# A new prologue, phi(k) ahead of its transpose, and DMA transposes in a fused attention and token-mixing kernel

## The chip, the core and the metric

The kernel runs on one core of a Trainium2 chip. A core has five instruction queues: TensorE (matmuls, PE in the profile), VectorE (DVE), ScalarE (ACT), GpSimd (POOL) and SyncE (SP, which here only issues transfers). They run independently and meet at semaphores. Transfers run on 16 DMA engines shared by all queues. Matmuls write PSUM, which has 8 banks of 128 x 512 float32; everything else lives in SBUF.

The metric is the device time of one execution in microseconds. The profile adds one profiled execution, whose span (first to last instruction) is a little shorter than its device time.

## What is computed

A residual block over 2048 tokens of width 1024: `x + A(layernorm(x)) + B(layernorm(x))`, all in bfloat16.

```python
def _A_ref(x, wq, wk, wv, wo, beta):            # 32 heads of 32, 4 segments of 512 tokens
    ...
    phi = lambda t: jnp.where(t > 0, t + 1.0, jnp.exp(t))
    ...
    for s in range(N):
        qs, ks, vs = (q[:, :, s].copy(), k[:, :, s].copy(), v[:, :, s].copy())
        logits = jnp.einsum('bhqd,bhkd->bhqk', qs, ks) * scale + mask
        p = _softmax(logits, axis=-1)
        a_dot = jnp.einsum('bhqk,bhkd->bhqd', p, vs)
        pq = phi(qs)
        num = jnp.einsum('bhld,bhde->bhle', pq, M)
        den = jnp.einsum('bhld,bhd->bhl', pq, z)[..., None] + 1e-06
        a_mem = num / den
        o = g * a_mem + (1.0 - g) * a_dot
        outs.append(o)
        pk = phi(ks)
        M = M + jnp.einsum('bhld,bhle->bhde', pk, vs)
        z = z + jnp.einsum('bhld->bhd', pk)
    ...
    return o @ wo

def _B_ref(x, w1, b1, w2, b2):
    h = _layernorm(x, axis=-1)
    u = jnp.einsum('bsd,sf->bdf', h, w1) + b1    # sums over the 2048 tokens, 3584 hidden
    u = _gelu(u)
    y = jnp.einsum('bdf,fs->bds', u, w2) + b2
    return y.transpose(0, 2, 1)

xn = _layernorm(x, axis=-1)
return x + _A_ref(xn, ...) + _B_ref(xn, ...)
```

A uses xn. B normalises xn once more (h). A needs xn with the model width on partitions (xnT); B's first product sums over tokens, so it takes h as it is, with tokens on partitions.

## The kernel before

The kernel is written with a small framework. `Res` objects record who wrote and who reads a buffer, and `fw.op`, `fw.group` (a run of matmuls) and `fw.dma` turn these into semaphore waits. Each engine runs its instructions in the order in which the Python code emits them. Two rules of the framework matter here: an engine other than TensorE that reads a PSUM bank also waits for other engines' earlier reads of that bank, and a DMA waits on the queue that issues it (SP, in order), so later transfers stand behind it.

Stages, in program order (`build`):

1. `consts`: SP issues the loads of x (16 chunks of 128 tokens, in pieces of 1, 1, 2, 4, 4 and 4 chunks), of beta and the two bias rows, and of the first two slices of w1 (1 MB each: all 2048 token rows by 256 hidden columns, so two hidden blocks "fc" of 128).
2. `norm_and_first_hidden`: a software pipeline over pairs of chunks. VectorE takes the statistics (`ln_stats`: two half rows and their aggregation) and the small arithmetic (`ln_small`, `ln_bias`) for both norms at once: the second one's factor follows from the first's variance. `ln_apply` writes normalised x into a temporary (VectorE for even chunks, ScalarE for odd ones) and h (GpSimd, all chunks). Two pairs later `x_transpose` turns the chunk with 8 TensorE transposes into PSUM, ScalarE copies it to xnT, and `early_hidden` adds the chunk's share to the sums of the first N_EARLY = 3 fc, in 6 banks: 6 matmuls a chunk.
3. `over_early` loads wv and the first wq and wk over the space of x; then `hidden` computes the other 25 fc: 32 matmuls each (16 chunks, two halves of 512 columns), each bank closed by a Gelu on ScalarE (`gelu`) into gT. w1 slices come through a ring of three.
4. `attention_and_out`: 32 units, each one segment of 512 tokens (4) by one group of four heads (8). Ahead of the units stand four v projections, q and k of units 0 and 1 (LEAD = 2), and `k_transpose(0)`. A unit u emits, in this order:
   - logits in three steps, each followed by an exponential on ScalarE (pT) and a causal select on GpSimd; the logits use banks 0 to 3, so each step needs the exponential before it;
   - between the steps, n0, n1 and n2 "main" matmuls (`main_emit`), that is, the MLP's second product (28 a half chunk) and, for fused chunks, the output projection (8 more); n3 more come at the end of the unit;
   - weighted sums (`weigh`, four query blocks, banks 4 and 5), the q projection two units ahead (bank 0), `o_transpose(u - 1)` (four TensorE transposes into bank 2, ScalarE copies to oT), `k_transpose(u + 1)` (four transposes of kT into bank 3; ScalarE Exp, then VectorE's two operations of `phi` write pk), the k projection (bank 1) and the v projection (bank 2).

   In segment 3 no k is transposed, since the memory is not updated any more. `combine(u - 1)` on VectorE makes the unit's output o_s. `weigh(u, 3)` uses pk to update the memory M. The main matmuls alternate between banks 6 and 7.
5. `tail` finishes the last four chunks; it holds the `o_transpose` of unit 31.

All transfers are issued from SP, the weights through rings (`_Ring`): w2 two pieces ahead, wq and wk one.

Of the kernel before, what the change touches and what calls it, by code (L numbers as in the profile page):

```python
# [18 lines left out]
P = 128  # L19
# [82 lines left out]
class FW:  # L102
    N_DMA_SEMS = 64
    N_OUT_SEMS = 40

    def __init__(self, nc, ctx):
# [14 lines left out]
        self.out_toks = []  # L121
        self._grp = None
# [76 lines left out]
    def dma(self, out_ap, in_ap, reads=(), writes=(), is_output=False, issuer="sp", extra=(),  # L199
            record_reads=True):  # L200
        es = self.E[issuer]
        if not is_output:
# [7 lines left out]
        ins = es.eng.dma_start(out_ap, in_ap)  # L210
        if is_output:
# [5 lines left out]
            self.out_toks.append(tok)  # L217
        else:
# [116 lines left out]
class _Kernel:  # L335
# [3 lines left out]
    N_EARLY = 3  # L339
# [7 lines left out]
    def build(self):  # L347
# [10 lines left out]
        def _(sp_eng):  # L358
            self.consts()
            self.norm_and_first_hidden()  # L360
            self.over_early()
# [6 lines left out]
    def alloc(self):  # L368
# [15 lines left out]
        self.ln_nb = a.take("ln_nb", [P, N_TCH, 2], F32)  # L384
# [11 lines left out]
        self.R_rs = [Res(f"rs{c}") for c in range(N_TCH)]  # L396
        self.R_vA = [[Res(f"vA{i}_{c}") for c in range(4)] for i in range(2)]
# [10 lines left out]
        self.xn_tmp = [e.take(f"xn_tmp{i}", [P, D_MODEL], BF16) for i in range(4)]  # L408
        self.early_end = e.at
# [4 lines left out]
        self.R_xnt = [Res(f"xnt{i}") for i in range(4)]  # L414
# [3 lines left out]
    def over_early(self):  # L418
        fw = self.fw
        e = _Arena(self.nc, self.early_base, self.early_end)  # L420
        wait = _after(*self.R_xin, *self.R_xnt)
# [73 lines left out]
    def consts(self):  # L495
        fw = self.fw
        self.load_x(0, 1)
        self.load_x(1, 1)
        fw.dma(self.beta_sb[:], self.A_beta.partition_broadcast(P), writes=[self.R_beta])
        self.load_x(2, 2)  # L500
# [3 lines left out]
        self.w1_ring.depth = 0  # L504
        self.w1_ring.ensure(0)
        self.load_x(4, 4)
        fw.dma(self.brow1[:], self.B_b1.rearrange("(c q) -> c q", q=P), writes=[self.R_brow1])
        fw.dma(self.brow2[:], self.B_b2.rearrange("(c q) -> c q", q=P), writes=[self.R_brow2])
        self.w1_ring.ensure(1)
        self.load_x(8, 4)  # L510
        self.load_x(12, 4)
        self.w1_ring.depth = 2
# [5 lines left out]
              reads=[self.R_ident], writes=[self.R_ident])  # L518

        fw.op("act", lambda e: e.activation(self.gcol[:], self.beta_sb[:], ACT.Sigmoid),  # L520
              reads=[self.R_beta], writes=[self.R_gcol])

    def load_x(self, c0, n):
        self.fw.dma(self.xin[:, c0:c0 + n, :], self.x_d[:, c0:c0 + n, :],
                    writes=[self.R_xin[c] for c in range(c0, c0 + n)])

    def late_consts(self):
# [7 lines left out]
        for i in range(2):  # L535
            fw.op("pool", lambda e: e.memset(self.vA[i][:], 1.0), writes=self.R_vA[i])
        gv = self.gcol[:].rearrange("p (g r) -> p g r", r=4)
# [4 lines left out]
        for row, R_row, col, R_col, n, b in ((self.brow1, self.R_brow1, self.b1c, self.R_b1c, N_FCH, 6),  # L542
                                             (self.brow2, self.R_brow2, self.b2c, self.R_b2c, N_TCH, 7)):
            with fw.group(reads=[R_row, self.R_ident], writes=[self.R_bank[b]]):
                fw.tp(self.bank_bf(b)[:, 0:n], row[0:n, :], self.ident[0:n, 0:n])
            fw.op("dve", lambda e: e.tensor_copy(col[:], self.bank_bf(b)[:, 0:n]),
                  reads=[self.R_bank[b]], writes=[R_col])


    def norm_and_first_hidden(self):  # L550
        fw = self.fw
        n_pair = N_TCH // 2
        for p in range(n_pair + 2):
            if p < n_pair:
                self.ln_stats(2 * p)
                self.ln_stats(2 * p + 1)
                self.ln_small(2 * p)
            if 1 <= p <= n_pair:
# [440 lines left out]
```

## Time and profile before

| what | us |
|---|---|
| median of 3 runs | 743.65 (743.56 to 743.65) |
| the profiled execution | 744.13 |
| its span | 742.3 |
| TensorE busy | 707.3 |
| ScalarE, VectorE, GpSimd busy | 280.4, 277.1, 112.5 |
| DMA: bytes moved, share of the 16 engines (main queue) | 65 MB, 37.5% |

In the views quoted below, a row of the timeline has start, length, engine, source line, operation, output, inputs, shapes and count; the brackets hold the idle time ahead of it and what ended that. "PEld" is a weight load; it runs ahead of the matmul that uses it. "SPq" is a transfer being issued by SP. Lines that belong to a helper (L188 all matmuls, L194 all transposes, L210 all transfers) are told apart by their tiles: w1s is the w1 ring, w2h the w2 ring, numbers tell the buffers of one ring apart. Matmul lengths overlap, because they are pipelined; the pace of a run is read from its starts, or from a window with a known count of instructions. Times that appear as "issue" have no recorded cause.

### The profile page before, as it was taken

To read this page: it belongs to the slowest core of one execution; us is meant where nothing else is said; L and a number is where in the kernel's file an instruction comes from. 1 tells how busy PE (TensorE), PEld (TensorE's weight loads), DVE (VectorE), ACT (ScalarE), POOL (GpSimd) and SP (SyncE) were. 2 spreads that over 40 slices of the span, in tenths; PEclk is the share of its full clock that TensorE was granted. 3 is DMA by queue.
4 is the path that set the end of the run, shared out by engine and by line. 5 is a ranking of instruction groups with operands and counts; after the bars stand their busy time and mean duration, and the time that the engine had idled before them with its cause. 6 is when DMAs were issued, how large, how long until landed. Compare 5 with 4: busy or idle time off the path is not lost.

```text
span 742.3 us, 11641 instructions
## 1 busy us (share of the span) xinstructions
PE 707.3 (95%) x5058; PEld 342.0 (46%) x5154; DVE 277.1 (37%) x617; ACT 280.4 (38%) x301; POOL 112.5 (15%) x154
## 2 busy tenths in 40 slices
PE   0999999999999999999999999999999999999996
PEld 0444444444444454454444455444455444444452
DVE  6930000000002234335454555554545554444543
ACT  2682121211212443544444343344444344443540
POOL 3640000000000221221121211121211112211220
PEclk9999999999999999999999999999999999999999
DMA  9429322323508141641615415052451606425003
GB/s 253 145 83 218 97 57 82 88 57 91 97 1 223 29 107 29 136 103 34 135 38 100 103 34 135 1 136 55 81 108 29 135 16 120 89 47 108 15 13 115
DMA packets 164603, 65.77 MB, mean 89 GB/s; under 512 B 125642, under 2 KB 156362, under 8 KB 164554
## 3 DMA queue, kind: packets, MB, share of 16 engines
q1 hardware_dynamic: 164554, 65.04, 37.5%
q8 instruction: 40, 0.66, 0.4%
q14 instruction: 9, 0.07, 0.0%
HBM read 59.79 MB, written 5.24 MB: 88 GB/s over the span
## 4 chain that ended last, share of the span: by engine, by line
PE 91%; DVE 4%; issue 1%; SPq 1%; ACT 1%; DMA 1%; POOL 0%; POOLq 0%; DVEq 0%
PE ps_all L188 89%; PE ps_all L194 2%; DVE ln_st L575 1%; SPq L210 1%; DVE ln_st L574 1%; DMA brow_51<-in_B_b_dram 1%; ACT pT L743 0%; DVE ln_mv L576 0%; POOL pT L749 0%; DVE xn_tmp_76 L607 0%; DVE ln_rs L584 0%; DVE fin_8030 L966 0%; DVE fin_8029 L966 0%; ACT xn_tmp_75 L604 0%; DVE xn_tmp_74 L607 0%
## 5 line engine op out<-in xcount | busy, mean ns | idle before, releaser
L743 ACT ACTIVATE pT<-ps_all 128x1536 bf16<-128x1536 f32 (+1 forms) x96 | 152.9, 1593 | 192.9 <-PE ps_all L188 192.9
L749 POOL TENSOR_SCALAR_AFFINE_SELECT pT<-pT 128x512 bf16<-128x512 bf16 x128 | 87.0, 692 | 585.1 <-ACT pT L743 585.1
L662 ACT ACTIVATE gT<-ps_all,b1c 128x512 bf16<-128x512 f32 x56 | 37.8, 689 | 134.5 <-PE ps_all L188 134.5
L710 DVE CAST vA_63<-ps_all 128x512 bf16<-128x512 f32 x16 | 11.1, 694 | 187.9 <-PE ps_all L188 187.7
L188 PE MATMUL ps_all<-h,w1s_79 128*128 128x512 bf16 x311 | 72.0, 382 | 2.7 <-issue 2.2
L188 PE MATMUL ps_all<-h,w1s_80 128*128 128x512 bf16 x314 | 72.3, 381 | 0.3
L188 PE MATMUL ps_all<-h,w1s_81 128*128 128x512 bf16 x251 | 55.6, 379 | 0.3
L188 PE MATMUL ps_all<-gT,w2h_663 128*128 128x512 bf16 x213 | 52.9, 380 | 1.1 <-issue 0.8
L188 PE MATMUL ps_all<-gT,w2h_662 128*128 128x512 bf16 x219 | 53.6, 381 | 0.3
L188 PE MATMUL ps_all<-gT,w2h_665 128*128 128x512 bf16 x214 | 53.0, 380 | 0.9 <-issue 0.6
L188 PE MATMUL ps_all<-gT,w2h_664 128*128 128x512 bf16 x218 | 53.3, 381 | 0.4 <-issue 0.2
L783 DVE CAST ost_1683<-ps_all 128x264 bf16<-128x264 f32 (+1 forms) x64 | 23.7, 391 | 71.8 <-PE ps_all L188 71.8
L783 DVE CAST ost_1684<-ps_all 128x264 bf16<-128x264 f32 (+1 forms) x64 | 23.7, 391 | 68.2 <-PE ps_all L188 68.1
L188 PEld LDWEIGHTS ps_all<-h,w1s_80 128*128 128x128 bf16 x320 | 31.4, 98 | 38.1 <-issue 0.6
L188 PEld LDWEIGHTS ps_all<-h,w1s_79 128*128 128x128 bf16 x320 | 30.7, 98 | 36.8 <-issue 3.0
L188 PEld LDWEIGHTS ps_all<-h,w1s_81 128*128 128x128 bf16 x256 | 25.0, 98 | 30.2
L188 PE MATMUL ps_all<-wo_sb,oT_1691 128*128 128x512 bf16 x126 | 32.4, 379 | 0.2
L188 PEld LDWEIGHTS ps_all<-gT,w2h_665 128*128 128x128 bf16 x224 | 20.6, 98 | 25.2 <-issue 2.5
L188 PEld LDWEIGHTS ps_all<-gT,w2h_663 128*128 128x128 bf16 x224 | 20.6, 98 | 25.2 <-issue 2.5
L188 PE MATMUL ps_all<-wo_sb,xnT_68 128*128 128x512 bf16 x127 | 30.5, 379 | 0.7 <-ACT xnT_68 L835 0.7
L188 PEld LDWEIGHTS ps_all<-gT,w2h_662 128*128 128x128 bf16 x224 | 19.3, 98 | 25.3 <-issue 6.4
L188 PEld LDWEIGHTS ps_all<-gT,w2h_664 128*128 128x128 bf16 x224 | 19.3, 98 | 25.3 <-issue 6.4
(167 smaller groups left out, 870.0 us busy)
## 6 DMA issues: line engine op xcount, KB each, us to landing
w1s_79<-in_B_w_dram SPq DMA_DIRECT2D x5, 1024.0 KB, 5.4
w1s_80<-in_B_w_dram SPq DMA_DIRECT2D x5, 1024.0 KB, 6.0
w1s_81<-in_B_w_dram SPq DMA_DIRECT2D x4, 1024.0 KB, 5.8
wq_658<-in_A_wq_dram SPq DMA_DIRECT2D x16, 256.0 KB, 3.0
wq_659<-in_A_wq_dram SPq DMA_DIRECT2D x16, 256.0 KB, 6.9
wk_660<-in_A_wk_dram SPq DMA_DIRECT2D x16, 256.0 KB, 2.9
wk_661<-in_A_wk_dram SPq DMA_DIRECT2D x16, 256.0 KB, 4.8
w2h_662<-in_B_w_dram SPq DMA_DIRECT2D x8, 448.0 KB, 4.9
```

The lines of the kernel that those rows point to most:

```text
L188: ins = self.nc.tensor.matmul(*args, **kwargs)
L194: ins = self.nc.tensor.transpose(out, in_, ident)
L210: ins = es.eng.dma_start(out_ap, in_ap)
L574: fw.op("dve", lambda e: e.bn_stats(st[:, 0:6], src[:, 0:512]), reads=[self.R_xin[c]], writes=[R])
L575: fw.op("dve", lambda e: e.bn_stats(st[:, 6:12], src[:, 512:1024]), reads=[self.R_xin[c], R], writes=[R])
L662: fw.op("act", lambda e: e.activation(self.gT[:, fc, half * 512:(half + 1) * 512], self.bank(b), ACT.Gelu_apprx_tanh, bias=self.b1c[:, fc: ...
L710: fw.op("dve", lambda e: e.tensor_copy(self.vA[i][:, c, :, 0:D_HEAD], self.bank(b).rearrange("p (h d) -> p h d", d=D_HEAD)), reads=[self.R ...
L743: fw.op("act", lambda e: e.activation(self.pT[:, :, off:off + total], self.ps[:, 0:4, 0:total], ACT.Exp, scale=SCALE), reads=self.R_bank[0:4],
L749: fw.op("pool", lambda e: e.affine_select(d, d, pattern=[[0, 4], [1, P]], compare_op=ALU.is_ge, fill=0.0, base=0, channel_multiplier=-1), ...
L783: fw.op("dve", lambda e: e.tensor_copy(dst, self.ps[:, b, 0:n * VW]), reads=[self.R_bank[b]], writes=[self.R_ost[o][qb]])
```

## The change

- **Loads.** The order is x0, first quarter of w1 slice 0, x1, first quarter of slice 1, x2 and x3, and then for each further quarter four chunks of x and the matching 512 rows of both slices (`load_w1_rows`). The two bias rows and beta are issued from ScalarE's queue.
- **Warm-up.** VectorE clears a buffer, ScalarE runs a square root on it, and TensorE runs 12 matmuls of zeros (N_WARM).
- **Order of the norm.** `NORM_ORDER` is a hand-written sequence. D is VectorE's statistics of a chunk, A and A' ScalarE's two passes for a chunk (sum, then squared differences; chunks 1, 4, 7, 10 and 13), S the factor of the second norm (two VectorE operations and a root on ScalarE), B its bias, h and g the scaling to h on VectorE (chunks 0, 2, 3) or GpSimd (the others).
- **Early hidden.** Four fc instead of three are summed as chunks come, in all eight banks: 8 matmuls a chunk, the last two chunks bank by bank.
- **Normalised x.** Its factor is taken for all 16 chunks at once after h; VectorE writes it over x (`xn_all`), and 16 DMA transposes write xnT, two at each fc from 4 to 11. The 128 TensorE transposes of x and ScalarE's copies go. `over_early` moves to fc 12 and `late_consts` behind the early matmuls.
- **phi(k) first.** phi is applied to k before its transpose: ScalarE Exp from the projection's bank, VectorE's two operations into mtmp; pk is then written by a DMA transpose, issued by SP after the third logits step. `o_transpose` becomes `o_transpose_dma`, issued at the same place; the one in `tail` stays on TensorE.
- **Order in a unit.** After the first two weighted sums: q projection, third sum, v projection, fourth sum, k projection. v is evicted by ScalarE instead of VectorE. n0, n1, n2 become 9, 7, 6 (segment 0) and 10, 8, 8, and n3 grows from 4 to 6 and from 7 to 10.

```diff
@@ consts
+        for q in range(4):
+            for c0, n in (((0, 1), (1, 1), (2, 2)) if q == 0 else ((4 * q, 4),)):
+                self.load_x(c0, n)
+                if c0 != 2:
+                    i = c0 if q == 0 else 0
+                    self.load_w1_rows(i, q)
+            if q:
+                self.load_w1_rows(1, q)
...
+        with fw.group(reads=[self.R_warm], writes=[self.R_bank[0]]):
+            for _ in range(self.N_WARM):
+                fw.mm(self.bank(0), self.warm[:, 0:P], self.warm[:], start=True, stop=True)
...
+    NORM_ORDER = ("D0 A1 S0 h0 A1' D2 S1 B1 g1 S2 h2 D3 A4 A4' S3 h3 D5 S4,5 D6 B4,5 g4 g5 A7 A7' D8 S6,7 B6,7 g6 g7 "
+                  "D9 A10 A10' S8,9 D11 B8,9 g8 g9 S10,11 D12 B10,11 g10 g11 A13 A13' D14 S12,13 D15 B12,13 g12 g13 "
+                  "S14,15 B14,15 g14 g15")
...
+        self.rstd(0, N_TCH, 0)
+        for c in range(N_TCH - 2):
+            self.early_hidden(c, c + 1, range(8))
+        for b in range(8):
+            self.early_hidden(N_TCH - 2, N_TCH, (b,))
+        self.late_consts()
...
+    def stats_act(self, c, second):
...
+            fw.op("act", lambda e: e.activation(self.junk[:], src, ACT.Identity, accum_out=sm[:, 0:1]),
+                  reads=[self.R_xin[c]], writes=[R, self.R_junk])
+            fw.op("act", lambda e: e.activation(sm[:, 1:2], sm[:, 0:1], ACT.Copy, scale=1.0 / (32 * D_MODEL)),
+                  reads=[R], writes=[R])
+            fw.op("act", lambda e: e.activation(self.ln_mv[:, c, 0:1], sm[:, 0:1], ACT.Copy, scale=1.0 / D_MODEL),
+                  reads=[R], writes=[R])
+        else:
+            fw.op("act", lambda e: e.activation(self.junk[:], src, ACT.Square, bias=sm[:, 1:2], scale=-1.0 / 32,
+                                                accum_out=self.ln_mv[:, c, 1:2]),
+                  reads=[self.R_xin[c], R], writes=[R, self.R_junk])
...
+    def xn_transpose(self, c):
         s, cc = c // 4, c % 4
+        self.fw.dma(self.xnT[s][:, :, cc * P:(cc + 1) * P], self.xin[:, c, :], reads=[self.R_xin[c]],
+                    writes=[self.R_xnT[c]], transpose=True, own=True)
...
@@ proj_k
+        if u // N_GRP < N_SEG - 1:
+            fw.op("act", lambda e: e.activation(self.etmp[1][:], self.bank(b), ACT.Exp),
+                  reads=[self.R_bank[b]], writes=[self.R_etmp[1]])
+            self.phi(self.mtmp[1][:], self.R_mtmp[1], self.kT[k][:], self.R_kT[k], 1)
...
+    def k_transpose(self, u):
+        j = u % 2
+        self.fw.dma(self.pk[j][:], self.mtmp[1][:], reads=[self.R_mtmp[1]], writes=[self.R_pk[j]], transpose=True)
...
+    def o_transpose_dma(self, u):
+        s, g, o = u // N_GRP, u % N_GRP, u % 2
+        self.fw.dma(self.oT[s % 2][:, g, :].rearrange("p (q t) -> p q t", q=4),
+                    self.o_s[o][:].rearrange("p q j -> p (q j)"),
+                    reads=[self.R_os[o]], writes=[self.R_oT[s % 2][g]], transpose=True)
...
@@ attention_and_out
-            n0, n1, n2 = (10, 8, 6) if s == 0 else (11, 9, 9)
+            n0, n1, n2 = (9, 7, 6) if s == 0 else (10, 8, 8)
...
             self.logits(u, 2)
+            if u + 1 < N_UNIT and (u + 1) // N_GRP < N_SEG - 1:
+                self.k_transpose(u + 1)
+            if u:
+                self.o_transpose_dma(u - 1)
             self.main_emit(n2)
             self.weigh(u, 0)
             self.weigh(u, 1)
             un = u + self.LEAD
             if un < N_UNIT:
                 self.proj_q(un, 0)
-            if u:
-                self.o_transpose(u - 1, 2)
-            if u + 1 < N_UNIT and (u + 1) // N_GRP < N_SEG - 1:
-                self.k_transpose(u + 1, 3)
             self.weigh(u, 2)
-            if un < N_UNIT:
-                self.proj_k(un, 1)
-            self.weigh(u, 3)
             m = u // 4 + 1
             if m < 2 * N_SEG:
                 self.proj_v(m, u % 4, 2)
+            self.weigh(u, 3)
+            if un < N_UNIT:
+                self.proj_k(un, 1)
             self.main_emit(n3)
```

More of the change, by code (lines that the diff above doesn't have):

```diff
@@ L121, in __init__ @@
         self.out_toks = []
+        self.own_sems = [ctx.enter_context(nc.semaphore(name=f"s_own{i}"))
+                         for i in range(self.N_OWN_SEMS)]
+        self.own_next = 0
         self._grp = None
@@ L413, in alloc @@
         self.R_xin = [Res(f"xin{c}") for c in range(N_TCH)]
-        self.R_xnt = [Res(f"xnt{i}") for i in range(4)]
+        self.R_junk, self.R_warm = Res("junk"), Res("warm")
         self.R_h = [Res(f"h{c}") for c in range(N_TCH)]
```

232 lines of the change are left out of this document (112 added, 120 removed).

## The prediction

> **What bounds the kernel now.** I read the page first: shares, slices and the chain.
>
> ```profile
> span 742.3 us, 11641 instructions
> PE 707.3 (95%) x5058; PEld 342.0 (46%) x5154; DVE 277.1 (37%) x617; ACT 280.4 (38%) x301; POOL 112.5 (15%) x154
> ...
> PE   0999999999999999999999999999999999999996
> ...
> PEclk9999999999999999999999999999999999999999
> ...
> PE 91%; DVE 4%; issue 1%; SPq 1%; ACT 1%; DMA 1%; POOL 0%; POOLq 0%; DVEq 0%
> ```
>
> The chain of waits is 91% TensorE, with a full granted clock. An edit pays only if it starts TensorE's work earlier, takes work from it, or removes one of its gaps. Next I cut the span into windows.
>
> ```profile
> 0.00:51.10 51.10, 30.74 (x223) 17.29 (x228) 34.98 (x97) 28.65 (x36) 25.47 (x26) 1.00 0.51 145
> 51.10:237.40 186.30, 185.41 (x848) 84.47 (x864) 3.47 (x5) 40.99 (x60) 0.00 (x0) 1.00 0.40 105
> ...
> 253.50:367.20 113.70, 112.86 (x949) 55.56 (x965) 45.96 (x116) 52.31 (x51) 19.98 (x32) 1.00 0.41 88
> 367.20:625.40 258.20, 255.23 (x2073) 125.75 (x2111) 135.27 (x285) 108.53 (x110) 44.91 (x64) 1.00 0.37 79
> ```
>
> Columns: window, length, busy time of PE, weight load, DVE, ACT, POOL, then clock, DMA share, GB/s. The second window is the rest of the MLP's first product and the four v, two q and two k projections: 864 weight loads in 186.3 us, or 0.2156 us for one 128x512 matmul, gapless. The first window is the prologue, where VectorE (35.0 of 51.1 us) is busier than TensorE. The last two are the attention units, near 99% busy: 113.7 us for eight, 14.21 each (segment 0), and 258.2 us for sixteen, 16.1 each (segments 1 and 2). So there are two places to gain: the start of the dense stage, now at 51.1 us, and TensorE's instructions in the units.
>
> **The prologue.** Before, 96 of the 896 matmuls of the first product are done by 51.1 us. After, 128 are done when the early part ends, at a time T1. The gain is 51.1 - T1 + 32 x 0.2156 = 58.0 - T1. T1 needs the prices of the new steps:
>
> ```profile
> 3.45 0.69 DVE L574 BATCH_NORM_STATS2 ln_st<-xin 128x6 f32<-128x512 bf16 x1 [3.45 <-DMA xin<-in_A_x_dram]
> ...
> 5.03 0.64 DVE L574 BATCH_NORM_STATS2 ln_st<-xin 128x6 f32<-128x512 bf16 x1
> ...
> 8.10 0.20 ACT L588 ACTIVATE ln_rs<-ln_rs 128x4 f32<-128x4 f32 x1
> ...
> 12.56 0.13 DVE L594 SCALAR_TENSOR_TENSOR ln_nb<-ln_mv,ln_rs 128x4 f32<-128x4 f32 x1
> ...
> 12.73 0.55 DVE L607 TENSOR_SCALAR xn_tmp_74<-xin,ln_rs,ln_nb 128x1024 bf16<-128x1024 bf16 x1
> 12.79 1.22 ACT L604 ACTIVATE xn_tmp_75<-xin,ln_nb,ln_rs 128x1024 bf16<-128x1024 bf16 x1
> 12.89 2.64 POOL L609 TENSOR_SCALAR h<-xin,ln_rs,ln_nb 128x1024 bf16<-128x1024 bf16 x2 [11.36 <-DVE ln_nb L594]
> ```
>
> VectorE statistics of a chunk (D) take 5.03 - 3.45 = 1.58 us. ScalarE statistics (A, A') are two passes at 1.22 and two small copies at 0.2: 2.84 us. Their accumulating output is in no row; I add nothing, at most another 0.2 a pass. S is two small VectorE operations and a root, 0.4 + 0.25; B is 0.13; h is 0.55 on VectorE or 1.32 on POOL (2.64 for two). Eight matmuls a chunk are 1.72 us on TensorE.
>
> When the data arrives:
>
> ```profile
> 0.00:10.00 10.00, 0.00 (x0) 0.00 (x0) 4.70 (x11) 3.00 (x4) 0.70 (x6) 1.00 0.77 186
> 10.00:20.00 10.00, 2.50 (x13) 1.40 (x14) 8.28 (x30) 1.56 (x4) 6.47 (x7) 1.00 1.11 340
> ```
>
> By 10 us 1.86 MB had moved, then 0.34 MB/us. In the new order x4 to x7 are complete after 2.62 MB: at 12.2 us, with 0.8 us for the signal 13.0. The three small transfers moved to ScalarE's queue stay on the same engines, so I keep the curve.
>
> The written order then gives, from 13.0: A4 and A4' end at 15.85; the root of S3, behind them on ScalarE, 16.1; h3 16.7; D5 18.3; S4,5 and D6 20.3; B4,5 and POOL's start 20.6; h4 21.9 us. From there POOL (1.32 a chunk), VectorE (two D and the S and B of three chunks, some 4.8 us, 1.6 a chunk) and ScalarE are all a little faster than TensorE's 1.72, so TensorE ends last: 21.9 + 12 x 1.725 + 0.1 = **T1 = 42.7 us, gain 15.3**. Chunks 0 to 3 are done near 19, leaving TensorE idle for almost 3 us.
>
> What is hidden: the eight Gelu evictions start as each bank closes; the one that frees bank 0 ends before bank 7 closes. The table loads for root, Sigmoid and Gelu fall into ScalarE's idle time; without that cover they cost up to 2.6 us once. The 16 operations for normalised x (0.55 each, 9 us) lie on VectorE beside 165 us of matmuls, and their DMA transposes beside fc 4 to 11, some 55 us, ahead of later w1 slices in SP's queue.
>
> **The attention units.** Next the timeline of one unit of segment 1, and the start of unit 0.
>
> ```profile
> 474.91 0.39 PE L194 MATMUL ps_all<-ident,o_s_1685 128*128 128x128 bf16 x4
> ...
> 475.13 0.39 PE L194 MATMUL ps_all<-ident,kT_1675 128*128 128x128 bf16 x4
> 475.30 0.41 PEld L188 LDWEIGHTS ps_all<-vA_64,pT 128*128 128x128 bf16 x12
> 475.36 0.46 PE L188 MATMUL ps_all<-vA_64,pT 128*128 128x33 bf16 x12
> ```
>
> ```profile
> 237.38 0.39 PE L194 MATMUL ps_all<-ident,kT_1674 128*128 128x128 bf16 x4
> ...
> 239.51 0.39 PE L188 MATMUL ps_all<-qT_1671,kT_1674 32*128 32x512 bf16 x4 [1.74 <-DVE pk_1680 L673]
> ```
>
> Eight transposes take 475.36 - 474.91 = 0.45 us of TensorE, four 0.23. Units 8 to 22 lose both: 15 x 0.45 = 6.8. Units 23 to 29 lose o alone: 7 x 0.23 = 1.6. In units 30 and 31 the next instruction waits for POOL anyway: 0. At unit 0 the transpose and its 2.13 us go, but ScalarE now has k's exponential ahead of the first logits exponential, about 1 us later: gain 1.1.
>
> Fewer main matmuls cover each logits step (n0, n1). In segment 0, where cover is thinnest:
>
> ```profile
> 310.77 1.88 ACT L743 ACTIVATE pT<-ps_all 128x2048 bf16<-128x2048 f32 x1 [4.46 <-PE ps_all L188]
> ...
> 312.92 0.34 PE L188 MATMUL ps_all<-qT_1673,kT_1676 32*128 32x384 bf16 x4
> ```
>
> The exponential ends at 312.65, the next logits start at 312.92: 0.27, of which some 0.06 is the signal. One matmul less (0.22) just fits. In the other segments the gap is larger. The new end of a unit is q, v, then k, then n3. Bank 1 is read by VectorE (cast) and only then by ScalarE (Exp), as the framework orders two readers of one bank; the next logits write that bank.
>
> ```profile
> 252.53 1.03 PE L188 MATMUL ps_all<-gT,w2h_663 128*128 128x512 bf16 x4
> 252.73 0.69 DVE L710 CAST vA_64<-ps_all 128x512 bf16<-128x512 f32 x1 [0.90 <-PE ps_all L188]
> 253.49 0.10 PEld L188 LDWEIGHTS ps_all<-qT_1672,kT_1675 32*128 32x128 bf16 x4 [0.42 <-DVE vA_64 L710]
> ```
>
> Today one eviction of 0.69 holds the logits 0.1 us longer than the four matmuls from 252.53 (4 x 0.216) cover. After, two in a row end about 0.2 + 0.68 + 0.6 + 0.1 = 1.6 us behind k's last matmul; n3 covers 6 x 0.216 = 1.3 in segment 0, a stall of 0.3, and 10 x 0.216 = 2.16 elsewhere, none. So a unit of segment 0 gains 0.45 - 0.2 = 0.25; with unit 0's 0.03 the eight give 1.8. ScalarE gains v's eviction and loses oT's, about even; VectorE loses v's.
>
> **The new waits.** Attention gains 6.8 + 1.6 + 1.8 + 1.1 = **11.3 us** if no DMA transpose is late. SP issues k's behind VectorE's phi, o's behind the combination; behind these stand that unit's remaining loads of w2, wq and wk, of which the rings hold a unit's worth. phi(k) sits in one buffer, so VectorE's next phi, with the stage additions and the combination queued behind it, waits for k's transpose. It has nearly a unit, 15.6 us.
>
> ```profile
> q1 hardware_dynamic: 164554, 65.04, 37.5%
> ...
> stg_1694<-in_A_x_dram SPq DMA_DIRECT2D x5, 256.0 KB, 2.9
> ```
>
> No row has a DMA transpose. A packet costs 0.375 x 742.3 x 16 / 164,554 = 27 ns of one engine. A 128 KB transpose in 256-byte packets would be 512 x 27 ns / 16 = 0.9 us; in single elements (65,536 packets) 111 us. I take 3 us, the plain 256 KB load, as the object is a block move of similar size. Other traffic is 0.37 x 16.1 = 5.9 us a unit, so 5.9 + 2 x 3 fits into 15.6.
>
> [...]
>
> **Sum.** 15.3 + 11.3 = 26.6 us off the profiled execution's 744.13 (its span of 742.3 and 1.8 around it) is 717.5; that execution lies 0.5 above the median shown, so 717.0 to 717.5. Bounds: T1 may be 40 (data 2 us sooner, POOL and TensorE following) or 45 (0.2 a ScalarE pass; TensorE slow at its restart), attention may give 9 to 13.
>
> **Rivals.** 0.2% (1.5 us) is about what a measurement of this kernel tells from no change.
>
> 1. *The prologue gives less*: the written order puts S3's root behind A4', and each later S behind a ScalarE pass; with dearer passes or x later, the feed falls to 2 us or more a chunk and T1 to 48. For: three engines within 10% of the pace. Against: DMA at 340 GB/s has x in by 22 us. Time 723.
> 2. *The units gain nothing*: the serial readers of bank 1 or late phi cost what the transposes gave. For: the 0.1 us stall already there. Against: 2.16 us of cover in 24 of 32 units. Time 717.5 + 11.3 = 729.
> 3. *The DMA transposes become the bound* (slower). With X us of queue each, a unit is 2X + 5.9; beyond 15.6, at X = 4.9, VectorE waits for k's buffer and TensorE for VectorE. It ends above 744 once 23 x (2X - 9.7) exceeds 26.6, X = 5.4; at X = 8 it is 717.5 + 145 = 862. For: unknown price, one queue. Against: the sizes are those of 3 us loads.
> 4. *The change doesn't do what it says*: early matmuls start no earlier, as the weights' quarter blocks come behind x. T1 near 51, time 726. Against: the first quarters are among the first 1.05 MB, there by 8 us.
>
> **Chances.** Forecast 0.65 (713 to 722), rival 1 0.13, rival 2 0.11, rival 3 0.08, rival 4 0.03. The range to 729 keeps all but rival 3 and the tails. Faster 0.92, slower 0.07, same 0.01.
>
> **What would show it.** Right: dense matmuls without a gap from about 43 us; statistics ended by 33; no TensorE rows of the o or k transposes but unit 31's; units of 13.9, 15.6 and 15.4 us; DMA transposes landing in under 5 us. Wrong: VectorE idle on a DMA ahead of phi's first operation, TensorE waiting on ScalarE's k exponential in segments 1 and 2, or gaps over 0.5 us between chunks after h4.

## The result, and the profile after

The changed kernel takes **720.88 us** (median of 4 runs, 720.03 to 721.95) against 743.65 (743.56 to 744.31): ratio 0.9693, 95% interval 0.9676 to 0.9709. The forecast was 717.5 us, with 713 to 722 as its likeliest stretch and a range that reaches to 729: the time lies in both, 3.4 us above the forecast. The profiled execution took 721.95, the longest of the four; its span is 720.2.

Of the page after, the lines that answer to those of before:

```profile
span 720.2 us, 11218 instructions
PE 701.0 (97%) x4818; PEld 324.6 (45%) x4818; DVE 263.1 (37%) x577; ACT 276.7 (38%) x314; POOL 111.1 (15%) x151
PE   6899999999999999999999999999999999999996
PEclk9999999999999999999999999999999999999999
q1 hardware_dynamic: 211248, 76.43, 48.9%
PE 93%; DVE 3%; ACT 2%; DMA 1%; issue 1%; SPq 0%; POOL 0%; DVEq 0%; ACTq 0%
```

TensorE still sets the end, now 97% busy. The matmul counts (5058 and 4818) understate what went, because some matmul records of before are missing; the weight loads, one for each, fall from 5154 to 4818. These 336 are the 128 transposes of x, 96 of k and 124 of o, less the 12 of the warm-up. The first slice says 6 where it said 0, though it holds a warm-up on zeros too. To see where the 22.1 us of the span went I cut both traces at the first logits of units 0, 1, 8, 23 and 30. The windows of before (columns as in the prediction):

```profile
0.00:239.51 239.51, 216.51 (x1073) 101.95 (x1095) 40.12 (x105) 70.60 (x96) 25.47 (x26) 1.00 0.43 114
239.51:253.49 13.98, 13.77 (x114) 6.69 (x117) 3.72 (x10) 5.87 (x5) 2.50 (x4) 1.00 0.30 60
253.49:352.96 99.47, 98.74 (x828) 48.40 (x842) 40.06 (x102) 45.46 (x44) 17.48 (x28) 1.00 0.36 76
352.96:593.92 240.96, 238.25 (x1945) 117.86 (x1982) 126.45 (x268) 102.66 (x105) 41.80 (x60) 1.00 0.40 84
593.92:699.97 106.05, 104.95 (x840) 50.48 (x857) 48.84 (x98) 44.48 (x42) 19.64 (x28) 1.00 0.33 67
```

And after:

```profile
0.00:225.15 225.15, 216.43 (x974) 96.29 (x975) 39.73 (x92) 63.10 (x112) 20.17 (x23) 0.98 0.54 135
225.15:240.36 15.21, 13.90 (x114) 6.50 (x114) 4.75 (x12) 7.06 (x7) 2.50 (x4) 1.00 0.65 117
240.36:339.13 98.77, 96.89 (x785) 45.51 (x785) 36.44 (x96) 46.99 (x44) 18.43 (x28) 1.00 0.58 101
339.13:573.39 234.26, 234.26 (x1861) 111.15 (x1862) 118.01 (x253) 105.35 (x104) 44.71 (x60) 1.00 0.48 101
573.39:677.89 104.50, 104.50 (x829) 48.93 (x830) 46.27 (x93) 44.06 (x40) 19.64 (x28) 1.00 0.43 81
```

| part | before | after | gain | forecast |
|---|---|---|---|---|
| up to the first logits, without the 2.13 us gap of unit 0's k transpose | 237.38 | 225.15 | 12.2 | 15.3 |
| that gap, less the growth of unit 0 (13.98 to 15.21) | | | 0.9 | 1.1 |
| units 1 to 7, 14.21 to 14.11 each | 99.47 | 98.77 | 0.7 | 1.75 |
| units 8 to 22, 16.06 to 15.62 each | 240.96 | 234.26 | 6.7 | 6.8 |
| units 23 to 29 | 106.05 | 104.50 | 1.55 | 1.6 |

Units 30, 31 and the tail (42.33 and 42.31) are unmoved. Nearly all of the 4.5 us that are missing in this profile lies in two rows: the prologue (3.1) and units 1 to 7 (1.05). The 16 DMA transposes of x cost TensorE nothing: it is busy for all of the 179.67 us from 45.48 to the first logits.

**The prologue.** TensorE's rows from the end of chunk 3 on (start, length, and in brackets the idle time ahead and what ended it):

```profile
19.31 1.03 PE L192 MATMUL ps_all<-h,w1s_79 128*128 128x512 bf16 x4
23.08 1.02 PE L192 MATMUL ps_all<-h,w1s_78 128*128 128x512 bf16 x4 [2.74 <-POOL h L651]
23.94 1.75 PE L192 MATMUL ps_all<-h,w1s_79 128*128 128x512 bf16 x4
25.48 1.91 PE L192 MATMUL ps_all<-h,w1s_78 128*128 128x512 bf16 x4
27.18 1.19 PE L192 MATMUL ps_all<-h,w1s_79 128*128 128x512 bf16 x4
...
45.48 2.75 PE L192 MATMUL ps_all<-h,w1s_80 128*128 128x512 bf16 x12
```

T1, the start of the first matmul behind the 128 early ones, is 45.48. Chunk 4 starts at 23.08 where the forecast had 21.9, after TensorE has been idle for 2.74 us. The first four matmuls still take 0.86 us (23.08 to 23.94); then the pace falls, down to 1.70 us for four (25.48 to 27.18). The windows show the clock:

```profile
23.00:24.00 1.00, 0.92 (x5) 0.48 (x6) 0.70 (x4) 0.58 (x2) 1.00 (x1) 1.00 1.22 291
24.00:25.00 1.00, 1.00 (x4) 0.34 (x3) 0.96 (x3) 0.94 (x4) 0.90 (x2) 0.55 1.21 290
25.00:26.00 1.00, 1.00 (x4) 0.40 (x3) 0.93 (x3) 0.97 (x2) 1.00 (x2) 0.50 0.81 197
```

**Segment 0.** The end of unit 0 stands for the ends of units 1 to 7:

```profile
238.63 1.46 PE L192 MATMUL ps_all<-gT,w2h_912 128*128 128x512 bf16 x6
238.83 0.69 DVE L746 CAST kT_1572<-ps_all 128x512 bf16<-128x512 f32 x1 [0.90 <-PE ps_all L192]
239.62 0.60 ACT L749 ACTIVATE etmp_1584<-ps_all 128x512 bf16<-128x512 f32 x1 [2.55 <-DVE kT_1572 L746]
240.36 0.40 PE L192 MATMUL ps_all<-qT_1568,kT_1571 32*128 32x512 bf16 x4 [0.27 <-ACT etmp_1584 L749]
```

This is the stall that the forecast described: six matmuls of cover (238.63 to 239.93) against two readers of bank 1 in a row, until 240.22. Logits start 1.73 us behind the cover's start, 0.43 longer than 6 x 0.216.

### The profile page after: what moved, and what is told of

Its sections match the earlier page's. It is cut to its first block, busy times and chain, and to the rows that moved or that the text cites. A ratio compares the mean times of both kernels' runs of the same rounds, so it can differ in the third digit from the quotient of the medians.

```text
span 720.2 us, 11218 instructions
## 1 busy us (share of the span) xinstructions
PE 701.0 (97%) x4818; PEld 324.6 (45%) x4818; DVE 263.1 (37%) x577; ACT 276.7 (38%) x314; POOL 111.1 (15%) x151
## 4 chain that ended last, share of the span: by engine, by line
PE 93%; DVE 3%; ACT 2%; DMA 1%; issue 1%; SPq 0%; POOL 0%; DVEq 0%; ACTq 0%
PE ps_all L192 93%; DMA xin<-in_A_x_dram 1%; ACT etmp_1584 L749 1%; DVE kT_1570 L746 0%; DVE ln_st L606 0%; DVE kT_1572 L746 0%; DVE kT_1571 L746 0%; DVE ln_st L605 0%; ACT pT L786 0%; SPq L214 0%; DVE h L647 0%; ACT L749 0%; POOL h L651 0%; DVE fin_7771 L1016 0%; DVE fin_7770 L1016 0%
## 5 line engine op out<-in xcount | busy, mean ns | idle before, releaser
L792 POOL TENSOR_SCALAR_AFFINE_SELECT pT<-pT 128x512 bf16<-128x512 bf16 x128 | 90.9, 723 | 561.5 <-ACT pT L786 561.5
L192 PE MATMUL ps_all<-h,w1s_78 128*128 128x512 bf16 x320 | 73.9, 385 | 7.1 <-POOL h L651 3.5
L192 PE MATMUL ps_all<-h,w1s_79 128*128 128x512 bf16 x320 | 73.8, 385 | 0.0
L746 DVE CAST kT_1570<-ps_all 128x512 bf16<-128x512 f32 x11 | 7.6, 690 | 178.9 <-PE ps_all L192 178.9
L192 PE MATMUL ps_all<-gT,w2h_912 128*128 128x512 bf16 x224 | 56.3, 380 | 0.0
L192 PE MATMUL ps_all<-gT,w2h_914 128*128 128x512 bf16 x224 | 56.3, 380 | 0.0
L192 PE MATMUL ps_all<-h,w1s_80 128*128 128x512 bf16 x256 | 55.9, 379 | 0.0
L192 PE MATMUL ps_all<-gT,w2h_913 128*128 128x512 bf16 x224 | 53.9, 381 | 0.0
L192 PE MATMUL ps_all<-gT,w2h_911 128*128 128x512 bf16 x224 | 53.9, 381 | 0.0
L749 ACT ACTIVATE etmp_1584<-ps_all 128x512 bf16<-128x512 f32 x24 | 14.3, 597 | 58.1 <-DVE kT_1572 L746 20.7
L192 PEld LDWEIGHTS ps_all<-gT,w2h_912 128*128 128x128 bf16 x224 | 20.6, 98 | 25.2 <-issue 2.5
L192 PE MATMUL ps_all<-wo_sb,oT_1587 128*128 128x512 bf16 x128 | 30.2, 379 | 0.0
```

What stands on the lines that cost most here:

```text
L192: ins = self.nc.tensor.matmul(*args, **kwargs)
L746: fw.op("dve", lambda e: e.tensor_copy(self.kT[k][:], self.bank(b)), reads=[self.R_bank[b]], writes=[self.R_kT[k]])
L749: fw.op("act", lambda e: e.activation(self.etmp[1][:], self.bank(b), ACT.Exp), reads=[self.R_bank[b]], writes=[self.R_etmp[1]])
L792: fw.op("pool", lambda e: e.affine_select(d, d, pattern=[[0, 4], [1, P]], compare_op=ALU.is_ge, fill=0.0, base=0, channel_multiplier=-1), ...
```

## The experiments

My theories after the result: the prologue's shortfall is h of chunk 4, which stands behind D6 on VectorE, plus a half clock that follows TensorE's idle time; segment 0's is the serial reading of bank 1; unit 0's growth is ScalarE's work ahead of its first exponential; and the DMA transposes cost nothing. Every kernel differs from the changed one by the edit shown. The times are medians, with the ratio to the kernel before and its 95% interval.

**The changed kernel again**, beside the next three: no edit.

> The changed kernel once more, as the yardstick for the others of this batch: 720.0 to 722.0, since its runs so far span that. A time outside says that the chip, not an edit, moves the others too.

721.03 us (719.78 to 721.85), 0.9683 [0.9665, 0.9702]. The units are the same (the fifteen from 8 to 22 again take 234.26 us, 337.62 to 571.88), but the first logits start at 223.64, 1.5 us earlier: all the scatter lies ahead of them. What follows is therefore read from the units' lengths and the first logits rather than from the times alone.

**The old attention behind the new prologue.**

```
-            self.k_transpose(u + 1)
...
-                self.o_transpose_dma(u - 1)
...
+                self.o_transpose(u - 1, 2)
...
+                self.k_transpose(u + 1, 3)
...
+            n0, n1, n2 = (10, 8, 6) if s == 0 else (11, 9, 9)
```

> The new prologue with the attention units of before (TensorE transposes of o and k, phi behind k's transpose, old order, old n0, n1, n2, v evicted by VectorE). Theory (both parts gain, and add up): the first logits start near 227.3 us (12.2 sooner than before), units last 14.21, 16.07 and 15.61 us as before, time about 731.5: the prologue is worth 12, the units 10 to 10.5. Rival (the parts depend on each other, since the DMA transposes of x compete with the w1 slices, or since the earlier start is lost again in front of the first unit): under 729 or over 734.

729.57 us (728.64 to 729.89), 0.9796 [0.9781, 0.981]. Units are back at 14.21, 16.06 and 15.61. The attention part is thus worth 729.57 - 721.03 = 8.5 us by the times, 9.9 by the traces (0.9 + 0.7 + 6.7 + 1.55). The difference lies ahead of the first logits, where the profiles scatter: at 224.69 they still hold unit 0's transpose gap, and they are 14.8 earlier than before's 239.51, against an expected 12.2. With unit lengths as in the kernel before, the two halves add up, and neither hides the other.

**Main matmuls between the steps as before.**

```
-            n0, n1, n2 = (9, 7, 6) if s == 0 else (10, 8, 8)
+            n0, n1, n2 = (10, 8, 6) if s == 0 else (11, 9, 9)
```

> Only n0, n1, n2 go back to 10, 8, 6 and 11, 9, 9, so n3 is 4 and 7 as before, behind k as the last projection. Theory (two readers of bank 1 in a row, 1.73 us, must be covered by n3): segment 0 has 4 x 0.216 = 0.86 us of cover, units of 14.11 + 0.43 = 14.54; segments 1 and 2 have 1.51, units of 15.62 + 0.22 = 15.84; segment 3 keeps 15.39. In all 7 x 0.43 + 15 x 0.22 = 6.3 us more, 727. Rival (the matmuls taken from between the logits steps are missed there, and their place at the end is worth nothing): the time falls or stays.

726.67 us (725.68 to 727.48), 0.9758 [0.9743, 0.9773]. The windows of units 1 to 7 and 8 to 22:

```profile
241.13:342.87 101.74, 95.93 (x770) 45.51 (x785) 36.46 (x96) 46.97 (x44) 18.37 (x28) 1.00 0.49 98
342.87:578.87 236.00, 232.82 (x1825) 111.62 (x1862) 118.13 (x253) 105.28 (x104) 50.83 (x60) 1.00 0.48 100
```

14.53 a unit in segment 0, up by 0.42, two matmuls of cover (2 x 0.216); 15.73 in the others, up by 0.11, half of what was expected there. What n0 and n1 give up becomes cover at the unit's end, where the two readers of bank 1 stand: the smaller n0 and n1 are part of the gain.

**The exponential of k from kT instead of the bank**, so that only the cast reads bank 1 (it then sees k rounded to bf16).

```
-            fw.op("act", lambda e: e.activation(self.etmp[1][:], self.bank(b), ACT.Exp),
-                  reads=[self.R_bank[b]], writes=[self.R_etmp[1]])
+            fw.op("act", lambda e: e.activation(self.etmp[1][:], self.kT[k][:], ACT.Exp),
+                  reads=[self.R_kT[k]], writes=[self.R_etmp[1]])
```

> ScalarE takes the exponential of k from the cast copy kT in SBUF instead of from bank 1, so the bank is free after VectorE's cast. Theory (in segment 0 the next logits wait 0.44 us for the second reader of bank 1): units 1 to 7 last 13.7 instead of 14.11 us, other segments keep 15.62 and 15.39; in all 2.5 to 3 us less, 718. Rival (the logits wait there for ScalarE itself, which must finish k's exponential before the next logits exponential, or for the clock of the cover): 14.0 or more a unit, time 720 or more.

718.26 us (717.64 to 719.38), 0.9659 [0.9645, 0.9674], 2.6 below the changed kernel's 720.88. The windows of unit 0 and of units 1 to 7:

```profile
225.47:240.14 14.67, 13.62 (x111) 6.46 (x113) 3.96 (x10) 6.96 (x7) 2.49 (x4) 1.00 0.67 121
240.14:336.56 96.42, 95.69 (x771) 45.29 (x784) 36.45 (x95) 47.22 (x45) 20.52 (x28) 1.00 0.58 103
```

The end of unit 0, as above:

```profile
239.68 0.63 ACT L749 ACTIVATE etmp<-kT 128x512 bf16<-128x512 bf16 x1 [2.49 <-DVE kT L746]
240.14 0.39 PE L192 MATMUL ps_all<-qT,kT 32*128 32x512 bf16 x4
```

Units 1 to 7 fall from 14.11 to 13.77. The exponential is no faster (0.63 us against 0.60) and ends at 240.31, but the logits no longer wait for it. The serial readers of the bank are shown to be segment 0's stall. Unit 0 falls too, by 0.54.

**Every DMA transpose issued twice**, the second into a spare tile.

```
+        self.fw.dma(self.spare[:], self.mtmp[1][:], reads=[self.R_mtmp[1]], writes=[self.R_spare], transpose=True)
...
+        self.fw.dma(self.spare[:], self.o_s[o][:].rearrange("p q j -> p (q j)"),
+                    reads=[self.R_os[o]], writes=[self.R_spare], transpose=True)
```

> Each DMA transpose of k and o in the units is issued a second time into a spare buffer that nobody reads; the two spare writes of a unit wait for each other, which adds to what stands in SP's queue. Theory (the transposes are hidden with room to spare: 2.4 to 6.1 us of 15.6): units of segments 1 and 2 stay within 0.05 of 15.62, the time rises by less than 1.5 us. Rival (the DMA transposes are near the bound, as the rival with a bound at 4.9 us of queue each has it): units longer by 1 us or more, time above 740.

720.64 us (720.52 to 720.78), 0.9678 [0.9663, 0.9692]: no change. The DMA issues (times, median us from issue to landing) and the window of units 8 to 22:

```profile
spare<-o_s SPq DMA_TRANSPOSE x31, 2.5
pk<-mtmp SPq DMA_TRANSPOSE x24, 4.1
spare<-mtmp SPq DMA_TRANSPOSE x24, 2.8
...
oT<-o_s SPq DMA_TRANSPOSE x16, 2.5
```

```profile
337.70:571.96 234.26, 231.89 (x1826) 111.18 (x1863) 118.09 (x253) 105.28 (x104) 44.62 (x60) 1.00 0.57 118
```

The DMA share rises from 0.48 to 0.57 and the units stay at 15.62: the transposes of k and o are hidden with room for as many again.

**Exp's table loaded early**, by a dummy exponential ahead of the preamble's q and k. In the changed kernel the load takes 1.28 us from 222.57.

```
+        fw.op("act", lambda e: e.activation(self.srec[:, 0, 0:1], self.gcol[:, 0:1], ACT.Exp),
+              reads=[self.R_gcol], writes=[self.R_srec[0]])
```

> One tiny Exp on ScalarE is put behind the v projections of the preamble, so that the table for Exp is loaded before k of unit 0 is cast; in the changed kernel the load of 1.28 us starts only when that cast is done. Theory (unit 0 is 15.21 us, 1.1 longer than units 1 to 7, because the table load and two exponentials of k stand ahead of its first logits exponential): unit 0 falls by 0.8 to 1.3 us, time about 720. Rival (unit 0 waits for VectorE's phi and the first DMA transpose of k instead): unit 0 within 0.3 of 15.21, no change.

720.82 us (720.04 to 721.37), 0.9694 [0.9678, 0.971]. Unit 0 is 15.04 us, 0.17 shorter: this theory fell. What does hold unit 0 is in ScalarE's timeline of the changed kernel, behind the first logits at 225.15:

```profile
226.21 0.60 ACT L749 ACTIVATE etmp_1584<-ps_all 128x512 bf16<-128x512 f32 x1 [1.26 <-DVE kT_1571 L746]
226.70 1.87 ACT L786 ACTIVATE pT<-ps_all 128x2048 bf16<-128x2048 f32 x1
```

The exponential of unit 1's k, which waits for VectorE's cast, stands ahead of unit 0's first logits exponential, which starts 1.55 us behind its logits. So:

**q and k ahead of v in the preamble**, which leaves 32 matmuls of v for k's cast and exponential.

```
-        for c in range(4):
-            self.proj_v(0, c, c)
         for u in range(self.LEAD):
-            self.proj_q(u, 4 + u)
-            self.proj_k(u, 6 + u)
+            self.proj_q(u, 2 * u)
+            self.proj_k(u, 2 * u + 1)
             if u == 0:
                 self.k_transpose(0)
+        for c in range(4):
+            self.proj_v(0, c, 4 + c)
```

> Ahead of unit 0 the two q and two k projections stand first, the four v projections last (banks swapped to match). Theory (unit 0 is 1.1 us longer than units 1 to 7 because the cast and the exponential of the k of unit 1 stand on VectorE and ScalarE ahead of unit 0's first logits exponential): with 32 matmuls of v between them, unit 0 falls from 15.2 to 14.1 to 14.5 us, units 1 to 7 stay at 14.1, first logits unmoved but for their scatter, time 719.5 to 721. Rival (unit 0 is long because its own phi and transpose, or the logits themselves, start from nothing): unit 0 stays at 15.0 to 15.2; or the four v evictions on ScalarE take the place of k's exponential and unit 0 gets longer, time 721 to 722.

720.66 us (719.35 to 721.38), 0.968 [0.9667, 0.9694]. The window of unit 0:

```profile
224.68:238.94 14.26, 13.91 (x114) 6.50 (x114) 2.39 (x8) 7.06 (x7) 2.50 (x4) 1.00 0.31 52
```

15.21 falls to 14.26, as expected, and the later units are unmoved. The gain of 0.95 us is too small to show in the times against the prologue's scatter.

**The second bias ahead of D6**, so that POOL starts h of chunk 4 sooner.

```
-    NORM_ORDER = ("D0 A1 S0 h0 A1' D2 S1 B1 g1 S2 h2 D3 A4 A4' S3 h3 D5 S4,5 D6 B4,5 g4 g5 A7 A7' D8 S6,7 B6,7 g6 g7 "
+    NORM_ORDER = ("D0 A1 S0 h0 A1' D2 S1 B1 g1 S2 h2 D3 A4 A4' S3 h3 D5 S4,5 B4,5 g4 g5 D6 A7 A7' D8 S6,7 B6,7 g6 g7 "
```

> Only the order of the norm changes: B4,5 and POOL's g4, g5 stand ahead of D6 instead of behind it. Theory (TensorE idles 2.7 us ahead of chunk 4 because its bias waits behind D6 on VectorE, and that idle time also costs it the full clock): POOL's h of chunk 4 starts near 20.4 instead of 21.7 us, the idle time falls to about 1.4 us, the granted clock stays at 1.0 from there, and the dense stage starts 1.3 + 1.7 = 3.0 us sooner: 42.4 instead of 45.5 us, time about 718. Rival (the clock falls whatever the idle time, or POOL's later chunks become the feed): only 1.3 us or less, 719.5 or more, with the half clock still in the rows behind 24 us.

720.25 us (719.46 to 720.69), 0.9683 [0.9669, 0.9697]. TensorE's rows of chunks 1 to 3, 4 and on:

```profile
15.28 5.35 PE L192 MATMUL ps_all<-h,w1s 128*128 128x512 bf16 x24 [1.88 <-POOL h L651]
22.22 7.21 PE L192 MATMUL ps_all<-h,w1s 128*128 128x512 bf16 x31 [1.59 <-POOL h L651]
30.16 6.20 PE L192 MATMUL ps_all<-h,w1s 128*128 128x512 bf16 x27 [0.74 <-POOL h L651]
```

Chunk 4 starts 0.9 us earlier, the idle time falls to 1.59 and no half clock follows: that part of the theory holds. The expected 718 us does not. TensorE waits for POOL again at 30.16, though chunks 4 to 7, 32 matmuls 0.2157 us apart from 22.22, would have let it start at 29.12: about 1.0 us is given back. The work on VectorE is as much as before; D6 only stands later in it. First logits at 223.64, as in the unedited kernel's other profile; the time is not told apart from it.

**Dummy matmuls in the idle time**: twelve on zeros behind chunk 3, added to an open sum in bank 0.

```
         for c in range(N_TCH - 2):
             self.early_hidden(c, c + 1, range(8))
+            if c == 3:
+                with fw.group(reads=[self.R_warm], writes=[self.R_bank[0]]):
+                    for _ in range(12):
+                        fw.mm(self.bank(0), self.warm[:, 0:P], self.warm[:], start=False, stop=False)
```

> Twelve matmuls of zeros are added into bank 0 behind chunk 3 (they add nothing to the sums), so TensorE is busy in most of its idle time ahead of chunk 4. Theory (idle time lowers the clock): matmuls of chunks 4 and 5 run at 0.216 us instead of 0.43, the dense stage starts at 43.8 instead of 45.5 us, time 719.2. Rival (the low clock comes from something other than idle time, for example the load that the dense matmuls begin with): the same 45.5, time unchanged at 720.9 or up to 2.6 us more, if the fillers delay chunk 4.

721.23 us (720.37 to 722.93), 0.97 [0.9685, 0.9715]. No half clock at chunk 4, but the twelve end at 24.5 and hold it back; first logits 224.88. The cure costs at least what it saves: the unedited kernel has 225.15 in one profile and 223.64 in the other. With **five** instead of twelve:

> Five dummy matmuls on zeros, in place of twelve, behind chunk 3: 1.1 us of TensorE at full clock. Theory (the granted clock halves for some 3.4 us after TensorE has been idle for about 2.7 us, and does not after 1.6 us): the idle time ahead of chunk 4 falls to about 1.6 us where it was 2.74, the matmuls of chunk 4 stand 0.216 us apart from the first, chunk 4 is not delayed, and first logits come at 200.4 us behind its first matmul, so 223.4 to 224 us and never 225 or later; time 720 or a little below, within the scatter of the runs. Rival (the half clock belongs to the chunk, to the DMA traffic or to the first use of those operands, not to the idle time): chunk 4 runs at 0.43 us a matmul all the same, first logits near 225.

720.57 us (720.43 to 720.81), 0.9687 [0.9671, 0.9703]. Chunk 4 starts at 23.22 at full clock, first logits 223.61, inside what was expected. It proves little, and neither do the twelve: in both profiles the half clock of chunk 0 lasted into chunk 1, to about 18.8 us, so that the 24 matmuls of chunks 1 to 3 took 7.16 and 7.31 us instead of 5.35, which closes most of the idle time by itself.

**One warm-up matmul instead of twelve** (N_WARM = 1).

> One warm-up matmul in place of 12. Theory (the warm-up is lost before its product is needed: after it TensorE is idle for 3.5 us, and the first chunk then runs at half clock with it as well; chunks 0 to 3 are in any case done before chunk 4 is there): first logits between 223.4 and 225.7 us, the scatter of the runs so far, time 720 to 722. Rival (the warm-up sets how fast chunks 0 to 3 run, and without it they end so late that chunk 4 has to wait for TensorE): chunk 4 starts after 24 us, first logits above 226 us, time 723 or more.

720.25 us (719.81 to 722.52), 0.9683 [0.9668, 0.9698]: no change. The first chunk's eight matmuls take 3.44 us, 0.43 each, half speed, as they do with twelve (3.39). The warm-up is lost in the idle time behind it: in the changed kernel's profile the twelve end at 6.56, full clock is recorded from 7.03 to 10.44, and chunk 0 starts at 10.79, at half clock.

Thirteen profiles share this prologue, edits aside. Chunk 4's first matmul, TensorE's idle time ahead of it, the clock behind it, and the first logits (us):

| profile | chunk 4 | idle ahead | clock behind | first logits | distance |
|---|---|---|---|---|---|
| changed kernel | 23.08 | 2.74 | half | 225.15 | 202.07 |
| exponential of kT | 23.40 | 2.73 | half | 225.47 | 202.07 |
| n as before | 23.64 | 2.74 | half | 225.72 | 202.08 |
| one warm-up | 23.62 | 2.73 | half | 225.69 | 202.07 |
| q, k ahead of v | 22.61 | 2.74 | half | 224.68 | 202.07 |
| changed kernel again | 23.25 | 0.79 | full | 223.64 | 200.39 |
| transposes twice | 23.32 | 0.73 | full | 223.71 | 200.39 |
| twelve dummies | 24.49 | none | full | 224.88 | 200.39 |
| five dummies | 23.22 | none | full | 223.61 | 200.39 |
| second bias first | 22.22 | 1.59 | full | 223.64 | 201.42 |
| three edits (below) | 22.20 | 1.58 | full | 223.63 | 201.43 |

Early table (no idle time at all, full clock, first logits 223.40) and old attention (0.25, full, with unit 0's gap) fit as well. At chunk 4 the half clock costs 202.07 - 200.39 = 1.68 us each time. There it came with an idle time of 2.73 us or more, in five profiles, and not with 1.59 or less, in eight. In six of these eight, chunk 0's half clock had lasted into chunk 1, which by itself shortens the idle time; in "second bias first" and "three edits" it is the edit that does, and they carry the argument.

**Three edits together**: the second bias ahead of D6, the exponential from kT, q and k ahead of v.

> The three edits that looked best, together: B4,5 with the h of chunks 4 and 5 ahead of D6, the exponential of k from kT instead of the bank, q and k projections ahead of v in the preamble. If they add up: units 1 to 7 at 13.77 (2.6 us with unit 0's share), unit 0 at 14 or below (another 0.6), first logits at 223.4 to 224.5: time 716.5 to 718. Rival (the edits overlap: unit 0 gains once only, and the prologue's scatter is as large as B4,5's gain): 718 to 719, no better than the exponential of kT alone.

**716.79 us** (715.61 to 716.93), 0.9626 [0.9613, 0.9639], the best of all. The windows up to the first logits, of unit 0, and of units 1 to 7:

```profile
0.00:223.63 223.63, 214.01 (x975) 95.50 (x976) 41.32 (x95) 63.27 (x112) 20.41 (x23) 0.98 0.57 141
223.63:237.55 13.92, 13.84 (x114) 6.47 (x115) 2.27 (x7) 6.93 (x7) 2.49 (x4) 1.00 0.29 52
237.55:333.97 96.42, 96.42 (x786) 45.31 (x786) 36.44 (x95) 47.20 (x45) 20.51 (x28) 1.00 0.58 103
```

Against the changed kernel's profile: 1.5 + 1.3 + 2.35 = 5.15 us, and its span is 5.1 shorter. Units 1 to 7 gain what the exponential from kT gained alone (2.35). Unit 0 gains 1.29, nearly the 0.54 and 0.95 of the two edits that touch it. The 1.5 ahead of the first logits can't be credited to the second bias: the unedited kernel's other profile has the same 223.64.

## Why the prediction was right, and where it was off

- **The structure held.** TensorE is the bound, the two places of gain are the two found, and they are additive: the old attention behind the new prologue loses only the attention's share. Within the prologue no run takes load order, ScalarE's statistics, the fourth fc and the transposes of x apart, so what each is worth stays open.
- **Units 8 to 29** were forecast at 8.4 us from the spacing of TensorE's own transposes (0.45 and 0.23 us) and gave 8.25. No instruction replaced what was taken out: PE is busy 234.26 of 234.26 us in the window of units 8 to 22.
- **The DMA transposes** were the unknown, between 0.9 and 111 us, taken as 3. By the medians of the rows they land in 2.4 to 6.1 us. The rows of k, and half of those of o:

```profile
pk_1576<-mtmp_1586 SPq DMA_TRANSPOSE x12, 2.5
pk_1577<-mtmp_1586 SPq DMA_TRANSPOSE x12, 6.1
oT_1587<-o_s_1581 SPq DMA_TRANSPOSE x8, 2.4
oT_1587<-o_s_1582 SPq DMA_TRANSPOSE x8, 3.5
```

  The list of waits (us in all, times, longest) has one wait for them, in unit 0:

```profile
DVE mtmp_1586 L717 <- DMA pk_1576<-mtmp_1586: 2.3, 1, 2.3
```

  Rival 3 is refuted by the doubling: four transposes a unit still hide. Of the signs listed, "under 5 us" fails for one buffer of pk (6.1), and VectorE was once idle on a DMA ahead of phi; neither held TensorE. On TensorE the same four 128x128 blocks took 0.23 us in the kernel before; from issue to landing a DMA transpose takes ten times that or more, but no engine that sets the end pays it.
- **The prologue's term was mis-sized**: 15.3 forecast, 12.2 measured in this profile, 12.2 and 13.7 in the profiles of the kernel and its repeat when the 2.13 us gap is set aside (first logits 225.15 and 223.64 against 237.38). The step that failed is "the written order then gives, from 13.0". Its chain began where x of chunks 4 to 7 arrives and took VectorE and ScalarE to be free by then. They were not:

```profile
13.72 1.20 POOL L651 TENSOR_SCALAR h<-xin,ln_rs,ln_nb 128x1024 bf16<-128x1024 bf16 x1 [12.20 <-DVE ln_rs L633]
21.73 4.86 POOL L651 TENSOR_SCALAR h<-xin,ln_rs,ln_nb 128x1024 bf16<-128x1024 bf16 x4 [6.81 <-ACT ln_mv L619]
```

```profile
11.19 0.69 DVE L605 BATCH_NORM_STATS2 ln_st<-xin 128x6 f32<-128x512 bf16 x1 [0.66 <-DMA xin<-in_A_x_dram]
...
14.04 1.16 DVE L647 TENSOR_SCALAR h<-xin,ln_mv,ln_rs 128x1024 bf16<-128x1024 bf16 x1 [0.27 <-ACT ln_rs L635]
15.12 0.67 DVE L605 BATCH_NORM_STATS2 ln_st<-xin 128x6 f32<-128x512 bf16 x1
...
17.43 0.55 DVE L647 TENSOR_SCALAR h<-xin,ln_mv,ln_rs 128x1024 bf16<-128x1024 bf16 x1 [0.27 <-ACT ln_rs L635]
```

  D2 starts at 11.19, when chunk 2 arrives. That chunk stands within the first 1.6 MB of the written order, but by 11.2 us 2.5 MB had moved (225 GB/s): counting bytes in the order of issue put this arrival too early. On ScalarE S2's root stands ahead of A4, which starts at 13.91 instead of 13.0. On VectorE h2 takes 1.16 us instead of 0.55, D3 starts only at 15.12, h3 ends at 17.98 where the forecast had 16.7, and POOL starts h4 at 21.73 instead of 20.6. That is 1.1 to 1.2 us of the 3.1 missing. Another 1.7 is the half clock, which the prediction held out only as a bound ("TensorE slow at its restart", T1 45; in the trace of before the weight loads from 19.24 to 20.95 stand 0.43 us apart, behind a TensorE idle time of 2.25) and left out of its sum; T1 came out at 45.48, past that bound. The remaining 0.3 lies in the dense stage, not followed further. The forecast's idle time of almost 3 us was right (2.74). The 0.8 us for the signal, in the 13.0 from which the chain starts, was an estimate, and no run shows it by itself: in the trace of before the first 0.26 MB, the size of a chunk of x, had moved by 2.8 us and the statistics of chunk 0 began at 3.45; in the changed kernel A4 stands behind S2's root, so its start does not show when chunk 4 arrived.
- **The pace after h4** was right: no gap between chunks and TensorE ending last, though its first matmuls ran at half clock.
- **Segment 0**: the mechanism (two readers in a row, six matmuls of cover) was right, the size not. The forecast took a stall of 0.3 and a gain of 0.25 a unit; the stall is 0.43 and the gain 0.10, so 0.13 of the 0.15 us missing in each of the seven units is the stall's size. Taking the second reader away gives 0.34 of it back.
- **Unit 0**: 1.1 forecast, 0.9 measured. The place was named (ScalarE has k's exponential first); it is unit 1's k, as the edit of the preamble shows.
- **Rival 1** was partly true: the prologue gave less, though not by a feed of 2 us a chunk. **Rival 2** is refuted by the lengths of units 8 to 29, **rival 4** by the early matmuls from 10.8 us on.

## What to carry to other kernels

When one engine sets the end, moving its transposes to DMA pays what they cost on that engine, as long as nobody waits: here 8.25 us in units 8 to 29, with 0.23 us a transpose on TensorE and 2.4 to 6.1 by DMA. Bound it by doubling the transfers (720.64 us against 720.88 here). Where two engines read one PSUM bank in turn and the next matmul writes that bank, let one of them read the copy that the other has made: 0.34 us a unit here. In a start-up chain, work every chunk from its own arrival through each queue, and price an idle time of TensorE at its length and the half clock that can follow it: here 2.74 us, and 1.68 us more.

## What the runs showed of the hardware

- At chunk 4 TensorE's half clock lasted 3.41 us in the changed kernel's profile (24.10 to 27.51, by the trace's clock records) and 3.40 to 3.42 by the windows of the other four profiles that have it there. Around chunks 0 to 2 it lasted 3.41 us in the changed kernel's (10.44 to 13.86), and 10.24 with five dummies (8.56 to 18.80, one idle time of 1.29 among them) and with the early table (10.52 to 20.76, one of 1.76 among them). Why it lasts longer in some profiles than in others stays open; ahead of chunk 4 it hardly moves the end, since it fills TensorE's idle time: chunk 4 starts at 23.08 in the changed kernel's profile and at 23.25 in the repeat's, where the half clock lasted to 19.16.
- Where the half clock began varied. At chunk 4 it began 0.04 to 1.3 us after TensorE had started again. Early in the profile with five dummies it began at 8.56 us, 1.16 us behind TensorE's last instruction, which ended at 7.40.
- Ahead of the first clock record the profile reads 1.00, also where the matmuls ran at half pace: in the changed kernel's the first record comes at 7.03 us, behind a warm-up of 5.30 us, 0.44 a matmul; in that of before at 21.60, behind the weight loads 0.43 apart; with one warm-up the windows from 10 to 11 and from 12 to 13 us read 1.00, and the eight matmuls of chunk 0, from 10.46, took 0.43 each.
- A VectorE tensor-scalar over 128x1024 took 1.16 us while POOL ran the same operation (from 13.72, 1.20 us) and 0.55 alone (from 17.43). One of before that started 0.16 us ahead of POOL's (12.73 against 12.89) took 0.55 too. The statistics beside POOL's later rows kept their 0.69 (from 22.17, POOL busy from 21.73 to 26.59). This was seen, not tested.
- An accumulating ScalarE pass is followed by a read of its own: 0.19 to 0.20 us in each of the ten rows of the changed kernel's profile, which the prediction had as its upper bound.
